# Window attention into a mixture of attention experts: scores as 64-key products, one transfer a unit for q and k, all masks on GpSimd, the gate in PSUM, new step lists

## The chip, the cores and the metric

The kernel runs on one core of a Trainium2 chip. The metric is the device time of one execution in microseconds. Engines are named as in the profile: PE is TensorE (PEld its weight loads), DVE VectorE, ACT ScalarE, POOL GpSimd, SP SyncE, which only issues transfers here.

## The reference

Two attentions follow one another. The first is a sliding window of 32 to either side over 8 batches x 8 heads x 576 positions x 64 dimensions, in fp32:

```python
scores = scale * np.matmul(q, k.transpose(0, 1, 3, 2))
mask = np.abs(pos[:, None] - pos[None, :]) <= 32
attn = softmax(np.where(mask, scores, -1e9))
x = (attn @ v) -> (8, 576, 512)
```

The second is a mixture of four causal attention experts on x: a gate `logits = x @ w_gate` picks the best two of four experts per position and weighs them by a softmax over the two; each expert computes `q, k, v = x @ wq[e], x @ wk[e], x @ wv[e]` (head dimension 64), causal softmax attention over all 576 positions, and a projection `@ wo[e]` back to 512. The output is the weighted sum, (8, 576, 512).

## The kernel before

**The order is written out.** The string ORDER lists 917 steps. A step's name gives its function, its batch and further indices, after a colon an engine (v DVE, g POOL, a ACT), after @ the PSUM banks it uses. The program walks the list once and emits each step's instructions on their engines; every engine runs its own instructions strictly in that order and waits by semaphores for what it needs. A load also waits for the last PE instruction that stands before it in the list (`load` adds that dependency), so a load does not run ahead of its place. PSUM is one tensor of eight banks; who holds a bank follows from the list.

**Window attention of batch b, unit (b, g) with g a group of four heads:**

- `lq`, `lk` load q and k of a unit, `lv` loads V. For q and k the unit's tile has 128 partitions, 32 for each head. `load_qk` knows two layouts. The one used throughout here lays rows 64 m + 2 p + o on partition p, and issues four transfers, one a head, with runs of 512 bytes; for batch 0 in two parts (rows 0 to 319 and 320 to 575). Part letters: `t` issues from ACT's queue, no letter from SP's. The other layout (letters `e`, `f`) lays rows 18 p + o on partition p; then a unit is one contiguous transfer with 4,608 bytes a partition. It is in the code and unused by the list.
- `tq`, `tk` (L298): DVE transposes 32 x 32 blocks, two instructions a unit and tensor, so that the 32 partitions of a head hold half of the head dimension and the columns are positions in order. The output's inner step is 2 elements (18 in the other layout).
- `sc(b, g, half)`: scores, transposed, for half the query columns (288): keys on PSUM partitions, queries as columns; four heads on four row groups of the array (32 rows of a half head dimension), one PSUM bank a head, two accumulating products for the two halves `dh`. Each fp32 product is two PE instructions. Block lists BLK say which keys meet which queries: an entry (par, m, n, lo, hi) takes n keys from 128 m + 64 par against columns lo to hi, on PSUM partitions from 64 par.
- `ex` (L336): ACT takes the exponential of two banks (128 x 576) into SBUF. `mk` (L340): multiplication by the window's mask, on POOL or DVE as the list says.
- `av`: probabilities times V with a column of ones, `un` divides (DVE), `xt` transposes on PE, `xf` copies out of PSUM, `xb` casts to bf16. `vc` copies values on chip so that each 64-key block has its neighbour.

**Experts of batch b,** pair j of experts: `ga` gate logits, `gt`, `ge`, `gm`, `gu` the choice and weights (small tensors of 20 columns; transposed logits LT, differences L2, exponentials EX and numerators NU in SBUF); `pp`/`pe` project q and k, `pv`/`ve` v; `ps` scores, `xe` exponential on ACT, `se` (L511) causal part zeroed on POOL; `po` values, `oe` (L544 to L546) division and gate weight; `pt`, `ot` transposition; `py`, `ye`, `st` output.

All matmuls are recorded at L179, PE transpositions at L182, loads at L185, copies at L171 (ACT) and L173 (DVE, POOL).

**Around the change.** The list starts with `s_mask s_pads lq100`, so the q of batch 1 goes first on SP; the first score step is sc010 and the first value product av02. Buffers hold three units of q and k and of probabilities.

Of the kernel before, what the change touches and what calls it, by code (L numbers as in the profile page):

```python
# [32 lines left out]
    cw0:g av03@2 av04@0 mk1011:g un04@0 sc111@46 un03@2 ex1111@6 cw1:v xt02@0 lw2 cw2:g xt01@2 xf01:v@2 xb01:v  # L33
    lq200 lk200 xf02:a@0 xb02:v mk1001:g ex1110@4 xt00@6 xf00:a@6 sc110@04 ga0@6 gt0@6 xb00:a ex1101@4 lv10
    pp001@2 lv12 ex1100@0 mk1100:g lv11 lq210 pp000@0 pe000:v@0 pe001:a@2 pp010@2 pe010:v@2 mk1101:g mk1111:g
    ps003@0 ps000@4 xe003@0 se003 ps002@6 pv00@0 xe000@4 xe002@6 pp011@4 tq200 vc11:g ve00:a@0 pe011:a@4 ps001@6
    xe001@6 tk200 sc200@02 ex2001@2 ps013@4 lv14 xe013@4 mk1110:v lk210 vc10:v lk300 ps010@6 xe010@6 ex2000@0 ge0
    mk2000:g sc201@24 se000 ex2011@4 ex2010@2 se001 ps012@6 tq210 av12@0 mk2011:g un12@0 av10@4 mk2010:g lq300
    pv01@3 xe012@6 ve01:a@3 gm0 lk310 av13@6 av11@0 un10@4 un13@6 un11@0 se012 av14@4 un14@4 tk210 xt11@6 lw3
    xf11:a@6 lv23 xb11:g xt12@0 xf12:v@0 xb12:g xt10@4 lv22 mk2001:g xf10:v@4 xb10:v lv20 ps011@2 xe011@2 sc211@06  # L40
    ex2111@6 ex2110@0 mk2110:v se002 sc210@24 pp110@6 ex2100@2 mk2100:g ex2101@4 lv21 lq310 cw3:g pe110:a@6 gu0
    mk2101:g pp101@2 pe101:a@2 po00@6 pp100@2 tk300 lv24 oe00@6 pp111@4 se011 pt00@6 pe100:v@2 ps102@2 ps103@0
    pe111:a@4 xe102@2 xe103@0 tq300 ga1@7 gt1@7 lq400 ot00:a@6 mk2111:v sc301@24 ex3010@2 ex3011@4 ge1 tk310
    sc300@06 ex3001@6 ps100@2 xe100@2 lk400 tq310 vc21:g se010 av23@4 vc20:g av22@6 un23@4 ex3000@0 pv11@2 un22@6
    ve11:a@2 av20@0 un20@0 av24@7 lk410 un24@7 se013 ps111@4 xe111@4 mk3011:g ps101@2 lv31 xe101@2 av21@0 un21@0
    sc311@46 ex3110@4 tq400 lv30 sc310@02 ex3111@6 xt21@4 lq410 lv44 ex3100@0 mk3100:g ex3101@2 mk3101:g tk400
    xt20@0 xf21:v@4 xt22@2 po01@6 xf20:a@0 xf22:v@2 ps110@4 oe01@6 ps113@0 ga2@2 gt2@2 xb22:v xe113@0 lv33
    mk3110:v xe110@4 gm1 sc401@06 ex4011@6 mk3010:v tk410 lv32 tq410 ex4010@0 xb21:g sc400@24 mk3001:g lv34
    ex4000@2 mk4000:v lv41 ex4001@4 pv10@6 lv42 lq500 pt01@5 ot01:v@5 lv40 ve10:a@6 xb20:g pp200@3 pe200:a@3
    pp210@0 vc30:a pp201@6 gu1 pe210:a@0 pe201:v@6 pv20@4 ps203@6 lk500 ve20:v@4 ps112@0 mk3111:v xe203@6 xe112@0  # L50
    se100 gm2 ps200@2 xe200@2 mk3000:g lv43 vc31:g av31@6 pv21@5 ve21:v@5 un31@6 av30@0 mk4001:g av33@2 un30@0
    un33@2 mk4010:g lv53 se103 av32@4 un32@4 py02@0 ye02:a@0 av34@7 un34@7 lq510 py01@2 xt32@7 ye01:v@2 xf32:a@7
    xb32:v xt31@4 tk500 xf31:a@4 lk510 sc410@06 ex4100@0 sc411@24 ex4111@4 ex4101@6 py00@0 ex4110@2 vc41:g vc40:g
    se101 ye00:a@0 tq500 tq510 lv52 lv50 xt30@4 xf30:v@4 pp211@6 se102 po10@2 oe10@2 pe211:a@6 ps210@6 ps211@4
    ga3@0 gt3@0 lv54 xe210@6 xe211@4 sc500@26 ex5001@6 ex5000@2 se110 sc501@04 ex5011@4 mk4111:v ex5010@0 mk5001:v
    se112 se111 se113 po11@6 oe11@6 lk600 ps201@4 xb30:g mk4100:g lv51 mk4101:g ps212@2 xe201@4 xe212@2 av41@0
    un41@0 av40@6 ps213@4 xe213@4 mk4011:g un40@6 ge3 ps202@0 mk4110:g av44@2 lq600 tk510 se201 xe202@0 un44@2
# [12 lines left out]
    ex6111@4 pp500@6 pp501@0 pe500:a@6 se313 se310 pt21@2 ot21:a@2 po31@4 ps402@6 xe402@6 pe501:v@0 oe31@4 tq710  # L70
    sc701@02 ex7011@2 st10 ex7010@0 mk6011:v sc700@46 ex7000@4 ex7001@6 ga5@2 ps503@3 xe503@3 ps501@0 ps500@6
    gt5@2 lv74 xe501@0 py22@5 ye22:v@5 vc60:g mk6100:g av61@3 un61@3 pv51@0 ve51:v@0 se411 xe500@6 mk6111:g
    mk6110:g av63@1 un63@1 av62@3 pv41@0 ve41:a@0 un62@3 av60@6 un60@6 mk7001:g ps403@3 ps413@0 xe413@0 xe403@3
    se403 mk7011:g lv70 av64@2 un64@2 ps400@0 ps410@4 ps502@6 pv50@2 xe400@0 xe502@6 xe410@4 se401 se402 ve50:v@2
    xt60@6 xt61@4 lv72 xf60:a@6 pt31@3 xb60:a xt62@2 xf61:v@4 xf62:v@2 ot31:a@3 py20@6 xb61:a ye20:v@6 se400
    po40@0 pp510@2 pe510:a@2 vc70:a xb62:g st20 pt30@7 se410 oe40@0 se500 py21@5 ot30:v@7 ga6@4 gt6@4 gm6 se413
    ye21:a@5 st21 st22 gm5 sc710@02 ex7100@0 sc711@46 ex7110@4 mk7110:v pp511@0 ge5 mk7100:g py30@4 ex7101@2
    mk7101:v pe511:v@0 ex7111@6 mk7111:v vc71:g py31@2 po41@6 oe41@6 pp601@0 ye30:a@4 pp600@4 pe600:v@4 se501
    ye31:a@2 pe601:a@0 mk7000:v ps510@0 ps513@6 xe513@6 se513 st30 se502 pp610@2 xe510@0 pt41@4 pt40@5 pe610:a@2
    se503 ge6 ot41:v@4 ps601@0 ot40:v@5 xe601@0 mk7010:g ps602@6 ps600@2 av71@4 un71@4 xe600@2 av70@0 se601 pv61@2  # L80
    ve61:a@2 un70@0 se600 av73@4 xe602@6 py42@0 py32@1 av72@2 un73@4 ye32:v@1 ps512@4 xe512@4 ps511@6 un72@2
# [14 lines left out]
def kernel(  # L96
# [20 lines left out]
    NQT = 5  # L117
# [194 lines left out]
    def vc(c, b, par):  # L312
# [317 lines left out]
```

## Time and profile before

| | |
|---|---|
| device time, three runs | 266.94, 266.94, 265.85 us (median 266.94) |
| span of the profiled execution | 262.5 us (its own device time is not given; the median is 4.4 us more) |
| PE busy | 228.9 us (87%) |
| DVE / ACT / POOL busy | 193.2 / 147.0 / 127.2 us |
| granted PE clock, mean | 0.975 |
| transfers | 89362 packets, 40.60 MB, 155 GB/s |

Busy time of PE is the union of pipelined matmuls whose ends are modelled, so PE may be busy and yet not at its peak. In the groups of instructions the columns are: line, engine, operation, output<-inputs, shapes, count | busy us, mean ns of one | idle us of the engine just before them and what ended it.

### The profile page before, as it was taken

Reading aid. Unit: us, or ns where it says so; the run is one execution under the profiler, and the core shown is the slowest. Engines: PE = TensorE matmul, PEld = TensorE weight load, DVE = VectorE, ACT = ScalarE, POOL = GpSimd, SP = SyncE. Lnnn points to the kernel's source line nnn. Section 1 sums busy time; section 2 is a strip of 40 time slices with the busy share of each in tenths; the row PEclk is TensorE's granted clock in tenths of the full one; section 3 lists DMA queues with packets and bytes.
Section 4 is the critical chain, followed back from the end, with each engine's and each line's share of the span. In section 5 each row is a group of like instructions: output and inputs, shape, how many; then the busy total and the mean of one; then the engine's idle time right before and its main releaser. Section 6 shows DMA issues by size and latency. Waiting matters only on the chain.

```text
span 262.5 us, 11479 instructions
## 1 busy us (share of the span) xinstructions
PE 228.9 (87%) x5013; PEld 183.2 (70%) x5024; DVE 193.2 (74%) x400; ACT 147.0 (56%) x221; POOL 127.2 (48%) x165
## 2 busy tenths in 40 slices
PE   0286999985989999699989999998899989999981
PEld 0165898664768888567878877886688758877650
DVE  2455896759899889998997956986876596667640
ACT  0223416761646557326745677776657657785852
POOL 5019706765686097337967906109734236322400
PEclk9995699999999999999999999999999999999997
DMA  8969989999974598886186798990021520124366
GB/s 166 209 171 180 228 160 211 204 198 226 199 177 138 161 209 176 170 196 162 34 205 201 157 162 159 216 290 15 2 63 42 186 80 2 32 92 157 126 216 208
DMA packets 89362, 40.60 MB, mean 155 GB/s; under 512 B 47072, under 2 KB 84960, under 8 KB 89312
## 3 DMA queue, kind: packets, MB, share of 16 engines
q1 hardware_dynamic: 86752, 38.69, 64.4%
q10 hardware_dynamic: 2560, 1.18, 2.4%
q8 instruction: 39, 0.64, 1.1%
q14 instruction: 11, 0.09, 0.1%
HBM read 30.42 MB, written 9.44 MB: 152 GB/s over the span
## 4 chain that ended last, share of the span: by engine, by line
PE 64%; DVE 16%; DMA 9%; issue 3%; ACT 3%; SPq 2%; POOL 1%; ACTq 0%; DVEq 0%
PE PS L179 57%; PE PS L182 7%; DVE A L340 5%; DMA qn<-in_q_dram 4%; DMA kn<-in_k_dram 4%; SPq L185 2%; ACT A L336 2%; DVE Tkn L298 1%; DVE RG L545 1%; DVE OE L546 1%; DMA out_dram<-Y 1%; DVE XN L368 1%; POOL V L173 1%; DVE Tqn L298 1%; DVE VE L173 1%
## 5 line engine op out<-in xcount | busy, mean ns | idle before, releaser
L179 PE MATMUL PS<-Tqn,Tkn 32*64 32x96 f32 (+5 forms) x2048 | 63.6, 307 | 16.9 <-DVE Tqn L298 11.6
L340 POOL TENSOR_TENSOR A<-A,MASKP 128x576 f32<-128x576 f32 x41 | 59.2, 1458 | 33.1 <-ACT A L336 32.5
L179 PEld LDWEIGHTS PS<-Tqn,Tkn 32*64 32x64 f32 (+1 forms) x2048 | 51.9, 158 | 29.4 <-DVE Tqn L298 12.0
L336 ACT ACTIVATE A<-PS 128x576 f32<-128x576 f32 x64 | 38.9, 650 | 41.0 <-PE PS L179 41.0
L506 ACT ACTIVATE ATE<-PS 128x1024 bf16<-128x1024 f32 x48 | 47.4, 1023 | 8.4 <-PE PS L179 6.8
L511 POOL TENSOR_SCALAR_AFFINE_SELECT ATE<-ATE 128x256 bf16<-128x256 bf16 (+1 forms) x80 | 31.4, 413 | 39.6 <-ACT ATE L506 24.2
L179 PE MATMUL PS<-V,A 128*64 128x65 f32 (+1 forms) x1280 | 39.6, 222 | 3.8 <-DVE XN L368 2.4
L179 PEld LDWEIGHTS PS<-V,A 128*64 128x64 f32 (+1 forms) x1280 | 36.1, 132 | 7.5 <-DVE XN L368 2.9
L173 POOL COPY V<-V 64x2048 f32<-64x2048 f32 (+1 forms) x12 | 21.8, 1820 | 27.3 <-DMA V<-in_v_dram 21.9
L298 DVE STREAM_TRANSPOSE Tkn<-kn 128x576 f32<-128x576 f32 (+2 forms) x36 | 23.2, 686 | 8.4 <-DMA kn<-in_k_dram 7.3
L298 DVE STREAM_TRANSPOSE Tqn<-qn 128x576 f32<-128x576 f32 (+2 forms) x36 | 23.2, 686 | 7.6 <-DMA qn<-in_q_dram 6.6
L340 DVE TENSOR_TENSOR A<-A,MASKP 128x576 f32<-128x576 f32 x23 | 25.3, 1109 | 3.0 <-ACT A L336 3.0
L368 DVE TENSOR_TENSOR XN<-PS,RC 128x512 f32<-128x512 f32 x32 | 22.1, 691 | 1.1
L179 PE MATMUL PS<-WV,XTB 128*128 128x256 bf16 (+1 forms) x192 | 18.8, 255 | 1.1 <-DVE OTT L173 0.8
L179 PE MATMUL PS<-WO,OTT 128*128 128x512 bf16 (+1 forms) x85 | 18.2, 341 | 1.4 <-ACT OTT L171 0.7
L179 PE MATMUL PS<-XTB,WK 128*128 128x288 bf16 x128 | 18.3, 286 | 1.0 <-DVE QKE L173 1.0
L182 PE MATMUL PS<-ident,XN 128*128 128x128 f32 x144 | 18.1, 275 | 1.1 <-DVE XN L373 0.9
L171 ACT COPY Y<-PS 128x1024 f32<-128x1024 f32 (+1 forms) x17 | 13.7, 826 | 9.3 <-PE PS L179 8.3
L179 PE MATMUL PS<-XTB,WQ 128*128 128x288 bf16 x128 | 18.1, 287 | 0.0
L179 PE MATMUL PS<-QKE 64*128 64x64 bf16 (+4 forms) x192 | 16.8, 277 | 1.4 <-DVE QKE L173 1.2
L182 PEld LDWEIGHTS PS<-ident,XN 128*128 128x128 f32 x144 | 15.8, 141 | 3.1 <-DVE XN L373 1.7
L179 PEld LDWEIGHTS <-ATE 128*128 128x128 bf16 x480 | 16.4, 97 | 2.2 <-POOL ATE L511 0.8
(71 smaller groups left out, 279.8 us busy)
## 6 DMA issues: line engine op xcount, KB each, us to landing
V<-in_v_dram SPq DMA_DIRECT2D x32, 256.0 KB, 4.7
out_dram<-Y SPq DMA_DIRECT2D x16, 512.0 KB, 3.8
qn<-in_q_dram SPq DMA_DIRECT2D x56, 144.0 KB, 4.3
kn<-in_k_dram SPq DMA_DIRECT2D x56, 144.0 KB, 4.3
V<-in_v_dram SPq DMA_DIRECT2D x8, 128.0 KB, 4.2
out_dram<-Y SPq DMA_DIRECT2D x16, 64.0 KB, 2.6
kn<-in_k_dram ACTq DMA_DIRECT2D x8, 80.0 KB, 3.5
qn<-in_q_dram SPq DMA_DIRECT2D x8, 80.0 KB, 2.8
```

What stands on the lines that cost most here:

```text
L171: nc.scalar.copy(o, i)
L173: eng(c).tensor_copy(o, i)
L179: last_pe[0] = nc.tensor.matmul(*a, **kw)
L182: last_pe[0] = nc.tensor.transpose(*a)
L185: r = q_.dma_start(o, i)
L298: nc.vector.transpose(T[:, 64 * m0:64 * m1].rearrange("q (m p o) -> q m o p", p=32, o=2), n_[:, 2 * m0:2 * m1, 32 * dh:32 * dh + 32].rearr ...
L336: nc.scalar.activation(AT[(2 * b + g) % NAT_][half][p], two(b0)[:, :, 0:HS], EXP, scale=scale_att)
L340: eng(c).tensor_tensor(out=ap, in0=ap, in1=MASK[:, None, HS * half:HS * half + HS].to_broadcast([128, 2, HS]), op=MULT)
L368: nc.vector.tensor_tensor(out=XN[T // 2][:, T % 2, :].rearrange("p (g h d) -> p g h d", g=2, h=4), in0=u[:, :, :, 0:64], in1=rc[:, :, :, N ...
L506: nc.scalar.activation(chunk(A, ch), two(b0), EXP, scale=scale_moe)
L511: nc.gpsimd.affine_select(ap, ap, pattern=[[0, n], [1, w]], compare_op=IS_GE, fill=0.0, base=0, channel_multiplier=-1)
L545: nc.vector.tensor_tensor(out=rg, in0=GG[b % 2][:, 2 * j:2 * j + 2, :], in1=rg, op=MULT)
```

## The change

1. **Scores.** Every product has 64 keys. An entry of BLK becomes (par, m, dh, lo, hi), the two head halves are entries of their own, and entries of the lower and the upper 64 PSUM partitions stand in turn: with four row groups that is eight tiles of the array. A step has 40 products instead of 32; columns outside the window of a 64-key block are no longer computed.
2. **q and k.** From batch 1 on, every unit's q and k are loaded with letter `e`: one transfer each, and transposed with an output step of 18. Batch 0 keeps the four transfers a part.
3. **Masks.** All 64 `mk` steps are on POOL (41 before, 23 on DVE).
4. **Gate.** Transposed logits, differences, exponentials and numerators lie in free columns (192 to 432) of the gate's PSUM bank, which stays taken from `ga` to `gu`; LT, L2, EX and NU are gone. `oe` writes its reciprocal in place in PSUM.
5. **Lists.** ORDER is new throughout, with the same 917 steps but for engines and queues. Other moves in it: evacuations `pe` 23 on ACT and 9 on DVE (18 and 14 before); no wide cast `xb` on DVE (3 before), 10 on POOL (7 before); `vc` 12 on POOL and 4 on ACT (2 on DVE and 2 on ACT before); wide `ye` 8 on ACT and 8 on DVE (12 and 4 before). The mask and the pads are made after the first scores.

```diff
 ORDER = """
-    s_mask s_pads lq100 lk011:t tk011:t lk001:t tk001:t lq011 lq001 tq011 lq002 lk012:t lk002:t lq012 s_ones
-    sc010@02 lv02 lk100 lv01 lv03 s_warm tq001 sc000@46 ex0101@2 ex0001@6 mk0001:g ex0000@4 lv00 s_ident mk0101:g
-    tk002:t tk012:t tq002 sc001@24 ex0011@4 mk0011:g mk0000:g tq012 sc011@46 ex0111@6 tq100 tk100 mk0111:g lq110
-    ex0100@0 ex0110@4 vc00:v ex0010@2 mk0010:v lk110 sc101@06 mk0110:v ex1011@6 tq110 ex1010@0 mk1010:v lv04 lw1
-    sc100@24 vc01:g av02@0 tk110 lv13 ex1001@4 un02@0 mk0100:g av01@4 un01@4 av00@6 un00@6 lw0 ex1000@2 mk1000:v
...
+    lk011:t lq002 s_ones lq011 lq001:t lk001 tq011:v tq002:v tk011:v tq001:v tk001:v lk012:t lv00 lk002 s_warm tk012:v
+    tk002:v s_pads lk100:e sc010@02 lq012:t lv03 lq100:e lv02 sc000@46 ex0000@4 ex0100@0 ex0101@2 s_mask lv01 sc001@40
+    lq110:e lk110:e tk100:e lv04 tq012:v ex0001@6 lw0 sc011@26 ex0010@4 ex0011@0 tq100:e sc100@04 lw1 lk200:e lw2
+    mk0000:g mk0100:g mk0011:g mk0001:g ex0111@6 ex0110@2 lq200:e sc101@26 ex1001@4 tq110:e mk0010:g s_ident mk0101:g
+    vc00:g mk0110:g vc01:a mk0111:g av01@4 ex1010@2 ex1011@6 tk110:e lv13 un01@4 ex1000@0 av02@2 av00@6 un00@6 un02@2
...
-    GS = {nm: many(2, [128, NQT, 4], F32, nm) for nm in ("L2", "EX", "GE", "LZ", "PK", "NU")}
+    GS = {nm: many(2, [128, NQT, 4], F32, nm) for nm in ("GE", "LZ", "PK")}
...
-    BLK = [[(0, 1, 128, 96, 288), (0, 0, 64, 0, 96), (1, 0, 64, 0, 160), (0, 2, 64, 224, 288)],
-           [(0, 2, 128, 288, 416), (0, 3, 64, 352, 480), (1, 3, 64, 416, 576), (0, 4, 64, 480, 576)]]
+    BLK = [[(0, 0, 0, 0, 96), (1, 0, 0, 0, 160), (0, 0, 1, 0, 96), (1, 0, 1, 0, 160),
+            (0, 1, 0, 96, 224), (1, 1, 0, 160, 288), (0, 1, 1, 96, 224),
+            (0, 2, 0, 224, 288), (1, 1, 1, 160, 288), (0, 2, 1, 224, 288)],
+           [(0, 2, 0, 288, 352), (1, 2, 0, 288, 416), (0, 2, 1, 288, 352), (0, 3, 0, 352, 480),
+            (1, 2, 1, 288, 416), (0, 3, 1, 352, 480), (1, 3, 0, 416, 576),
+            (0, 4, 0, 480, 576), (1, 3, 1, 416, 576), (0, 4, 1, 480, 576)]]
...
-        for par, m, n, lo, hi in BLK[half]:
+        for par, m, dh, lo, hi in BLK[half]:
             k0 = 128 * m + 64 * par
-            for dh in range(2):
-                for hh in range(4):
-                    r = slice(32 * hh, 32 * hh + 32)
-                    mm(PS[64 * par:64 * par + n, bank[hh], lo - c0:hi - c0], K[dh][r, k0:k0 + n], Q[dh][r, lo:hi],
-                       start=(dh == 0), stop=(dh == 1), skip_group_check=True)
+            for hh in range(4):
+                r = slice(32 * hh, 32 * hh + 32)
+                mm(PS[64 * par:64 * par + 64, bank[hh], lo - c0:hi - c0], K[dh][r, k0:k0 + 64], Q[dh][r, lo:hi],
+                   start=(dh == 0), stop=(dh == 1), skip_group_check=True)
...
+    def gate(b0, n):
+        if n:
+            return PS[:, b0, 352 + 20 * n:372 + 20 * n].rearrange("p (t e) -> p t e", e=4)
+        return PS[:, b0, 192:352].rearrange("p (t x) -> p t x", x=32)
+
     def gt(c, b, b0):
         i = b % 2
-        nc.vector.transpose(LT[i][:, :, :], one(b0)[:, 0:160].rearrange("p (t x) -> p t x", x=32))
-        L = LT[i][:, :, 0:4]
+        nc.vector.transpose(gate(b0, 0), PS[:, b0, 0:160].rearrange("p (t x) -> p t x", x=32))
+        L = gate(b0, 0)[:, :, 0:4]
...
-        nc.vector.tensor_tensor(out=GS["NU"][i], in0=GS["EX"][i], in1=GS["PK"][i], op=MULT)
+        nc.vector.tensor_tensor(out=gate(b0, 3), in0=gate(b0, 2), in1=GS["PK"][i], op=MULT)
...
-        nc.vector.reciprocal(rg, p_[:, :, :, 64])
-        nc.vector.tensor_tensor(out=rg, in0=GG[b % 2][:, 2 * j:2 * j + 2, :], in1=rg, op=MULT)
+        nc.vector.reciprocal(p_[:, :, :, 64], p_[:, :, :, 64])
+        nc.vector.tensor_tensor(out=rg, in0=p_[:, :, :, 64], in1=GG[b % 2][:, 2 * j:2 * j + 2, :], op=MULT)
```

More of the change, by code (lines that the diff above doesn't have):

```diff
@@ L33 @@
[L33 to L57, printed above, removed]
@@ L92 @@
+    py70@2 py72@4 st62 ye70:a@2 ye72:v@4 st71 st70 st72
 """
@@ L436, in gm, with gu @@
         nc.vector.tensor_tensor(out=GS["PK"][i], in0=L, in1=bc(GV["m2"][i]), op=IS_GE)
-    def gu(c, b):
+    def gu(c, b, b0):
         i = b % 2
-        nc.vector.tensor_tensor(out=GS["NU"][i], in0=GS["EX"][i], in1=GS["PK"][i], op=MULT)
-        nc.vector.tensor_reduce(GV["su"][i], GS["NU"][i], axis=AXX, op=ADD)
+        nc.vector.tensor_tensor(out=gate(b0, 3), in0=gate(b0, 2), in1=GS["PK"][i], op=MULT)
+        nc.vector.tensor_reduce(GV["su"][i], gate(b0, 3), axis=AXX, op=ADD)
         nc.vector.reciprocal(GV["su"][i], GV["su"][i])
-        nc.vector.tensor_tensor(out=GG[i][:, :, :].rearrange("p e t -> p t e"), in0=GS["NU"][i],
+        nc.vector.tensor_tensor(out=GG[i][:, :, :].rearrange("p e t -> p t e"), in0=gate(b0, 3),
                                 in1=bc(GV["su"][i]), op=MULT)
```

103 lines of the change are left out of this document (62 added, 41 removed).

## The prediction

> **What bounds the kernel now.** I read the page first (span, busy shares, chain, costliest groups), then windows, then the chain in order of time.
>
> ```profile
> span 262.5 us, 11479 instructions
> PE 228.9 (87%) x5013; PEld 183.2 (70%) x5024; DVE 193.2 (74%) x400; ACT 147.0 (56%) x221; POOL 127.2 (48%) x165
> PE 64%; DVE 16%; DMA 9%; issue 3%; ACT 3%; SPq 2%; POOL 1%; ACTq 0%; DVEq 0%
> PE PS L179 57%; PE PS L182 7%; DVE A L340 5%; DMA qn<-in_q_dram 4%; DMA kn<-in_k_dram 4%; SPq L185 2%; ACT A L336 2%; DVE Tkn L298 1%; DVE RG L545 1%; DVE OE L546 1%; DMA out_dram<-Y 1%; DVE XN L368 1%; POOL V L173 1%; DVE Tqn L298 1%; DVE VE L173 1%
> L179 PE MATMUL PS<-Tqn,Tkn 32*64 32x96 f32 (+5 forms) x2048 | 63.6, 307 | 16.9 <-DVE Tqn L298 11.6
> ```
>
> PE is the bound: 87% busy, 64% of the chain that ended last. Its largest group is the scores, 63.6 us. The page gives no device time of its own execution; the runs beside it have a median of 266.94 us, 4.4 us more than the span. I sum against 262.5 and add 4.4.
>
> The timeline of PE shows where the value products begin, and windows cut there and at two places further on what the engines do (length, then busy of PE, PEld, DVE, ACT, POOL, then granted clock, DMA share, GB/s):
>
> ```profile
> 31.59 0.63 PE L179 MATMUL PS<-V,A 128*64 128x65 f32 x14
> ```
> ```profile
> 0.00:31.59 31.59, 16.76 (x384) 13.66 (x385) 17.12 (x45) 7.45 (x12) 16.12 (x22) 0.84 0.91 190
> 31.59:70.85 39.26, 34.48 (x856) 28.25 (x853) 30.38 (x55) 19.46 (x31) 21.25 (x23) 1.00 1.06 199
> 70.85:240.00 169.15, 161.68 (x3562) 130.78 (x3567) 135.84 (x276) 107.07 (x161) 85.81 (x109) 1.00 0.56 131
> 240.00:262.50 22.50, 16.00 (x221) 10.52 (x221) 9.88 (x29) 12.99 (x17) 4.04 (x12) 0.94 0.58 206
> ```
>
> Up to 31.59 the kernel does six of 32 score steps (384 of 2048 instructions) and mostly waits for loads. From 31.59 to 70.85 (the first products of batch 1's second expert group) PE has 4.8 us idle, with DVE at 77%. From 70.85 to 240 PE is 96% busy, 7.5 us idle: there only less PE work helps. The end is a chain through the last batch.
>
> **The score step.** It becomes 40 products of 64 keys instead of 32, two instructions each (2048 over 32 steps is 64). One pair of steps, cut where 128-key products change to 64-key products:
>
> ```profile
> 67.45:70.85 3.40, 3.40 (x128) 2.87 (x128) 0.00 (x0) 1.00 1.14 206
> 67.45:68.11 0.66, 0.66 (x16) 0.54 (x17) 1.00 0.84 230
> 68.11:69.13 1.02, 1.02 (x53) 0.90 (x49) 1.00 0.97 193
> 69.13:69.99 0.86, 0.86 (x19) 0.64 (x17) 1.00 1.31 227
> 69.99:70.85 0.86, 0.86 (x52) 0.79 (x49) 1.00 1.39 184
> ```
>
> A step is 1.70 us. The 128-key blocks have 128 and 192 columns and four turns each (two head halves, two instructions): 0.66 and 0.86 us. So 64 columns x 4 turns are 0.20 us, 0.78 ns a column and turn, and 0.26 us is entry. The 64-key stretches (48 instructions each) run the two output halves side by side; by the longer half they should take 0.26 + 224 x 4 x 0.78 = 0.96 (measured 1.02) and 0.26 + 160 x 4 x 0.78 = 0.76 (measured 0.86). Columns explain them up to 0.10.
> After the change either half of a step has 288 columns on each side (96+128+64 or 64+128+96 against 160+128): 288 x 4 x 0.78 = 0.90, one entry instead of two, 0.26, and 0.10 on top: 1.26 us, 0.44 less. Below lies 0.90 (no entry), above 2.13, if an instruction costs what the mean one of the pair does (80 x 3.40/128). I take 1.26, near the lower end, since columns explain all four stretches. 26 steps come after 31.59, so A = -11.4 us, bounds -20.8 and +11.2.
>
> [...]
>
> **The start.** The chain in order of time, and POOL's first masks:
>
> ```profile
> 1.26 3.93 DMA kn<-in_k_dram
> 5.57 2.95 DMA kn<-in_k_dram
> 8.54 2.75 DMA kn<-in_k_dram
> 11.30 2.85 DMA qn<-in_q_dram
> 14.80 3.13 PE PS L179 x48
> ```
> ```profile
> 18.68 1.41 POOL L340 TENSOR_TENSOR A<-A,MASKP 128x576 f32<-128x576 f32 x1 [13.91 <-ACT A L336]
> 20.93 4.16 POOL L340 TENSOR_TENSOR A<-A,MASKP 128x576 f32<-128x576 f32 x3
> ```
>
> Loads go in generations; four follow one another before the products at 14.80. Now SP begins with batch 1's q (lq100). In the new list that goes behind batch 0, and sc000 needs three generations: about 11.3, then two transpositions, a step and its exponential, 3.3: first mask at about 14.6 instead of 18.68. But all eight masks of batch 0, the identity (0.8, the hole in the second row pair) and a value copy now stand in POOL's one queue ahead of the first value product:
>
> ```profile
> L340 POOL TENSOR_TENSOR A<-A,MASKP x41: 1393/1413/1923, 18.7 to 218.7; 128x576 f32<-128x576 f32 x41
> L340 DVE TENSOR_TENSOR A<-A,MASKP x23: 709/750/2480, 27.1 to 216.7; 128x576 f32<-128x576 f32 x23
> L433 DVE TENSOR_TENSOR GE<-LT,m x8: 165/170/1461, 58.9 to 234.7; 128x20 f32<-128x20 f32 x8
> ```
> ```profile
> L173 POOL COPY V<-V 64x1536 f32<-64x1536 f32 x4 | 5.9, 1468 | 2.0 <-DMA qn<-in_q_dram 1.9
> L511 POOL TENSOR_SCALAR_AFFINE_SELECT ATE<-ATE 128x256 bf16<-128x256 bf16 x64 | 25.9, 427 | 24.8 <-ACT ATE L506 24.2
> L173 POOL COPY V<-V 64x2048 f32<-64x2048 f32 x8 | 16.0, 1996 | 25.3 <-DMA V<-in_v_dram 21.9 <-DMA qn<-in_q_dram 3.3
> L511 POOL TENSOR_SCALAR_AFFINE_SELECT ATE<-ATE 64x128 bf16<-64x128 bf16 x16 | 5.7, 355 | 14.8 <-ACT ATE L508 14.4
> L173 POOL CAST XTB<-XTF 128x1024 bf16<-128x1024 f32 x7 | 7.3, 1036 | 5.9 <-ACT XTF L171 4.0 <-DVE XTF L173 1.9
> L298 DVE STREAM_TRANSPOSE Tkn<-kn 128x576 f32<-128x576 f32 x28 | 20.0, 754 | 3.8 <-DMA kn<-in_k_dram 2.7 <-PE PS L179 1.1
> L336 ACT ACTIVATE A<-PS 128x576 f32<-128x576 f32 x64 | 38.9, 650 | 41.0 <-PE PS L179 41.0
> L220 DVE MEMSET QKE<- 128x64 uint32 x3 | 0.3, 112 | 0.0
> L213 DVE MEMSET V<- 128x64 f32 x2 | 0.2, 112 | 0.0
> ```
>
> 8 x 1.413 + 0.8 + 1.47 = 13.6, so the first value product at about 28.2: B = -3.4 us. Bounds -6 (it waits for the six steps alone) and +3 (the loads gain nothing, masks from 18.7 on without DVE's help: 32.3, and one late exponential).
>
> **Masks on POOL.** 23 masks leave DVE (23 x 1.109 = 25.5) and cost POOL 23 x 1.413 = 32.5 us. The POOL and DVE rows (minimum, median, maximum) show DVE instructions on two SBUF operands blown up from 0.17 to 1.46 and from 0.71 to 2.48. In the new kernel none is left: masks, casts and value copies leave DVE, and the gate's operands lie in PSUM. DVE comes to about 150 us. Where DVE's time goes from the path, POOL is late next. From first value product to first products of batch 1's second group, the new list has the same six score steps, ten value steps and transpositions, four projections of batch 0; PE has 34.48 - 6 x 0.44 = 31.8 us. POOL has 15 masks (21.2), three wide casts (3.1), two value copies (3.5), seven causal pieces (2.9), WQ's cast and the small ones (1.8): 32.5. POOL is the longer one there. I keep the idle 4.8 on top: 37.3 instead of 39.26, so this stretch gains 2.0, not 2.6. From 70.85 to 240 POOL has 41 masks (57.9) and some 50 us of the rest in 160 us; cover for PE is the lead of the units, so zero, bounds 0 and 7 x 1.41 x 2 (two late masks a batch).
>
> **Transfers and transpositions.** 112 issues of q and k become 28 from batch 1 on. Their waits on the chain after the start are two:
>
> ```profile
> 50.46 3.88 DMA qn<-in_q_dram
> 61.33 4.05 DMA qn<-in_q_dram
> ```
>
> PE runs on beside them but for tenths (4.8 us idle in all that stretch), so I book nothing, bounds -4 and 0. The transposition now writes every 18th element instead of every second. I keep 754 ns: setting 64 scattered elements (V's ones, 65 apart) took 112 ns, as long as 64 adjacent ones (QKE's pad). Upper bound: twice the time, 56 x 0.754 = 42 us of DVE.
> [...]
>
> **Gate, division, copies.** Gate operations at their undisturbed 0.17 cost DVE less; the PSUM bank stays taken through a chain of eight short operations, covered by seven other banks: zero. ACT gets five evacuations of q and k, two value copies and some small ones more and four output copies less:
>
> ```profile
> L171 ACT CAST QKE<-PS 128x576 bf16<-128x576 f32 x18 | 11.4, 641 | 9.0 <-PE PS L179 7.6 <-DVE su L441 1.4
> L171 ACT COPY V<-V 64x1536 f32<-64x1536 f32 x2 | 2.9, 1472 | 0.0
> L171 ACT COPY Y<-PS 128x1024 f32<-128x1024 f32 x12 | 12.0, 1015 | 4.7 <-PE PS L179 3.7 <-ACT ATE L506 0.9
> ```
>
> 5 x 0.64 + 2 x 1.47 - 4 x 1.02 = +2.1 of 147 us on an engine idle half the time: zero.
>
> **Sum.** 262.5 - 3.4 (start) - 2.0 (to 70.85) - 20 x 0.44 = 8.8 (to 240) - 0 (end) = 248.3; + 4.4 = 252.7 us.
>
> **Rivals.**
> 1. Instructions set the score's pace. For it: 2560 instead of 2048. Against it: 17.9 ns in the best stretch. At 26.6 ns a step is 2.13 us: 262.5 - 3.4 + 26 x 0.43 + 4.4 = 274.7, slower; it outweighs the start from 22.9 ns on. Chance 0.10. [...]
> 2. POOL's queue becomes the bound: causal pieces of one batch wait behind masks of the next. For it: 32.5 against 31.8 above; against it: 48% busy now. One late mask a batch, 7 x 1.41: 262.6; two: 272.4; slower from ten late masks in all. Chance 0.17, half of it slower.
> 3. ACT: two exponentials of a step (2 x 0.65 = 1.30) outlast it (1.26), so the banks of a pair come free late. At 0.7 us for eight pairs: 258.3. For it: today a step leaves 0.4 us; against it: ACT idle half the time. Chance 0.10.
> 4. Transpositions take twice as long; they hold 2% of the chain, so +5.3: 258.0. Chance 0.06. [...]
> 5. Otherwise as summed, 245 to 259: chance 0.57.
>
> A measurement of this kernel tells 0.5% from no change. Faster: 0.57 + 0.10 + 0.06 + half of rival 2, 0.81; same 0.04; slower 0.15. Low end: scores at 0.90 (-9.4) and the start's bound (-2.6) give 241; the high end reaches into rival 2: 266.
>
> **What will show it.** Score steps of 1.2 to 1.3 us and about 45 us in their group; first value product near 28; POOL near 160 us, masks near 1.41; transpositions at 0.75; no DVE mask; PE near 215 us. I am wrong if score steps stay at 1.7, if PE waits for masks (A on POOL) by more than a few us, or if the idle time in 70.85 to 240 grows.

## The result, and the profile after

| | time, median (lowest to highest) | profiled execution: its time, span |
|---|---|---|
| before | 266.54 us (263.76 to 268.46) | not given, 262.5 us |
| after | 270.39 us (266.24 to 277.34) | 272.21 us, 270.5 us |

The ratio of after to before is 1.0103, 95% interval 1.0063 to 1.0143: the change makes the kernel about 1% slower, where 252.7 us was forecast. Ratios, here and below, are over the fast executions alone (of after the ten of 20 that lie within 1.5% of its fastest, so not the profiled one), and medians are over all executions, which is why those of the table stand at 1.0144 to one another.

The page of the changed kernel: busy shares, the chain that ended last by engine and by line, then the rows of the masks, the scores and a transposition.

```profile
span 270.5 us, 12380 instructions
PE 224.7 (83%) x5526; PEld 180.3 (67%) x5536; DVE 172.4 (64%) x353; ACT 153.1 (57%) x241; POOL 156.1 (58%) x192
...
PE 72%; DMA 11%; issue 8%; DVE 4%; ACT 3%; ACTq 0%; SPq 0%; DVEq 0%
...
L341 POOL TENSOR_TENSOR A<-A,MASKP 128x576 f32<-128x576 f32 x64 | 89.5, 1413 | 37.5 <-ACT A L337 36.9
L177 PE MATMUL PS<-Tqn,Tkn 32*64 32x128 f32 (+3 forms) x2560 | 52.5, 297 | 28.7 <-issue 11.2
...
L292 DVE STREAM_TRANSPOSE Tkn<-kn 128x576 f32<-128x576 f32 x28 | 32.6, 1243 | 5.1 <-PE PS L177 3.2
```

PE has 4 us less work than before and yet the span is 8 us longer. DVE has 21 us less work, POOL 29 us more, and neither has much of the chain (DVE 4%, against 16% before; POOL none). What is new is "issue", 8% of the chain against 3% before: time in which the engine waited for nothing that the profile shows. Windows over two undisturbed stretches of scores (one step, then a pair) and over one disturbed step show what that is worth (length, busy PE and its instructions, granted clock, DMA share, GB/s):

```profile
99.40:100.69 1.29, 1.29 (x82) 1.00 0.81 304
120.50:122.98 2.48, 2.48 (x162) 1.00 0.05 10
144.80:148.90 4.10, 1.61 (x81) 1.00 0.89 303
```

Left alone, a step of 80 instructions takes 1.24 to 1.29 us, as forecast (1.26). The third takes 4.1 us, at full clock, with 1.61 us of work in it. The timeline of PE there, and the pieces of "issue" over 2 us in the chain of the changed kernel (start, length):

```profile
144.82 0.68 PE L177 MATMUL PS<-Tqn,Tkn 32*64 32x64 f32 x33
148.00 0.99 PE L177 MATMUL PS<-Tqn,Tkn 32*64 32x128 f32 x47 [2.49 <-issue]
```
```profile
26.96 3.46 issue
...
38.35 3.40 issue
...
81.49 2.11 issue
...
145.51 2.49 issue
```

PE stops in the middle of a step, with operands and banks in hand. The waits (us in total, times, longest), first of before, then of after, show in these rows crumbs of at most 0.4 us before and stops of up to 4.1 us after:

```profile
PEld PS L179 <- issue: 8.9, 36, 0.4
...
PE PS L179 <- issue: 0.2, 1, 0.2
```
```profile
PEld PS L177 <- issue: 25.9, 25, 4.1
...
PE PS L177 <- issue: 18.7, 14, 3.5
```

What PE waits for is its own program. The page's part on DMA queues has a row for it (kind "instruction"), which I had passed over: 39 packets before, 43 after. Its row in before, then the rows of after:

```profile
q8 instruction: 39, 0.64, 1.1%
```
```profile
q1 hardware_dynamic: 56736, 38.68, 52.1%
q10 hardware_dynamic: 2560, 1.18, 1.9%
q8 instruction: 43, 0.70, 1.1%
```

Each is a packet of 16,384 bytes, and PE (with PEld) executes 256 instructions between one and the next, so 64 bytes an instruction. In before, PE and PEld execute 10,048 instructions, 39.3 blocks of 256; in after 11,072, 43.3. From the packet records and the starts of PE's instructions (in us from the span's start), four of the blocks:

```
after, packet no. (from 0)       1              3              11             24
packet on its way          27.38-28.72    39.00-40.28    81.22-82.30   145.68-146.62
PE's start behind the hole     30.42          41.75          83.60          148.00
distance of PE's starts         3.93           3.62           2.38            2.76
```

In each PE runs dry about 449 instructions past the start of a block (counted from PE's first recorded instruction: in after at 449, 705, 961, 1217 and so on, always whole blocks of 256 further, to one instruction), and goes on 1.3 to 1.7 us after the late packet has landed. Below, a **hole** is a distance of over 0.35 us between two starts of PE without a semaphore wait that ends within 2 us of the landing of such a packet. Before has none. After has 13, together 22.0 us. The forecast span was 248.3 us; 248.3 + 22.0 = 270.3, and 270.5 was measured.

That these meet is partly luck, for other terms of the forecast are off too (below), and the granted clock costs time that neither number holds. Between 31.59 and 240 us before had the full clock, 1.00 in both rows of the prediction. In after four stretches of 3.41 us stand at half of it (length, busy PE, PEld, DVE, ACT, POOL, then granted clock, DMA share, GB/s):

```profile
43.34:46.75 3.41, 3.41 (x18) 3.22 (x16) 1.24 (x4) 1.85 (x2) 1.10 (x3) 0.50 0.00 0
84.30:87.71 3.41, 3.41 (x65) 3.41 (x66) 0.90 (x2) 1.72 (x4) 1.77 (x2) 0.50 0.89 164
149.16:152.57 3.41, 3.41 (x17) 2.14 (x15) 0.00 (x0) 1.75 (x3) 2.70 (x4) 0.50 0.13 31
179.88:183.29 3.41, 3.41 (x113) 2.79 (x100) 1.46 (x3) 1.51 (x3) 0.44 (x2) 0.50 0.02 5
```

PE is busy all through them. From one product of 288 columns (XTB with WQ) to the next the starts stand 240 ns apart there and 123 elsewhere (medians). If all of PE's work there went by the clock alone, they cost 4 x 3.41 x 0.50 = 6.8 us, an estimate. The first three begin 0.7 to 1.6 us behind the end of a hole of over 2.3 us, the fourth 0.8 us behind two waits of PE for a transposition (1.51 and 0.55 us). But none follows the longest hole (26.50 to 30.42), so what sets them off isn't shown. Over its 20 executions after was granted 0.928 (in the longest, 277.34 us) to 0.981; before, beside the runs below, 0.965 to 0.999.

### The profile page after: what moved, and what is told of

It reads as the page before. It is cut to its first block, busy times and chain, and to the rows that moved or that the text cites. A ratio compares the mean times of both kernels' runs of the same rounds, so it can differ in the third digit from the quotient of the medians.

```text
span 270.5 us, 12380 instructions
## 1 busy us (share of the span) xinstructions
PE 224.7 (83%) x5526; PEld 180.3 (67%) x5536; DVE 172.4 (64%) x353; ACT 153.1 (57%) x241; POOL 156.1 (58%) x192
## 3 DMA queue, kind: packets, MB, share of 16 engines
HBM read 30.42 MB, written 9.44 MB: 147 GB/s over the span
## 4 chain that ended last, share of the span: by engine, by line
PE 72%; DMA 11%; issue 8%; DVE 4%; ACT 3%; ACTq 0%; SPq 0%; DVEq 0%
PE PS L177 63%; PE PS L180 9%; DMA qn<-in_q_dram 4%; DMA out_dram<-Y 3%; DMA kn<-in_k_dram 2%; DMA V<-in_v_dram 1%; ACT A L337 1%; DVE Tkn L292 1%; DVE Tqn L292 1%; ACT Y L169 1%; DVE Y L171 0%; ACT VE L169 0%; ACTq L183 0%; ACT WV L169 0%; ACT WK L169 0%
## 5 line engine op out<-in xcount | busy, mean ns | idle before, releaser
L341 POOL TENSOR_TENSOR A<-A,MASKP 128x576 f32<-128x576 f32 x64 | 89.5, 1413 | 37.5 <-ACT A L337 36.9
L177 PE MATMUL PS<-Tqn,Tkn 32*64 32x128 f32 (+3 forms) x2560 | 52.5, 297 | 28.7 <-issue 11.2
L177 PEld LDWEIGHTS PS<-Tqn,Tkn 32*64 32x64 f32 x2560 | 44.9, 148 | 35.7 <-issue 19.1
L292 DVE STREAM_TRANSPOSE Tkn<-kn 128x576 f32<-128x576 f32 x28 | 32.6, 1243 | 5.1 <-PE PS L177 3.2
L292 DVE STREAM_TRANSPOSE Tqn<-qn 128x576 f32<-128x576 f32 x28 | 32.2, 1242 | 3.0 <-PE PS L177 1.9
L171 POOL CAST XTB<-XTF 128x1024 bf16<-128x1024 f32 (+1 forms) x18 | 12.5, 706 | 18.5 <-DVE XTF L171 6.9
L169 ACT COPY XTF<-PS 128x128 f32<-128x128 f32 (+1 forms) x23 | 13.4, 632 | 16.4 <-PE PS L180 13.3
L169 ACT CAST QKE<-PS 128x576 bf16<-128x576 f32 x23 | 14.4, 642 | 9.3 <-PE PS L177 9.1
L177 PE MATMUL PS<-VE,ATE 128*128 128x65 bf16 x480 | 17.5, 193 | 2.7 <-issue 1.5
L171 DVE COPY Y<-PS 128x1024 f32<-128x1024 f32 (+1 forms) x12 | 11.5, 956 | 12.7 <-PE PS L177 10.5
```

The lines of the kernel that those rows point to most:

```text
L169: nc.scalar.copy(o, i)
L171: eng(c).tensor_copy(o, i)
L177: last_pe[0] = nc.tensor.matmul(*a, **kw)
L292: nc.vector.transpose(T[:, :].rearrange("q (p o) -> q o p", o=18)[:, o0:o1], n_[:, o0:o1, 32 * dh:32 * dh + 32])
L341: eng(c).tensor_tensor(out=ap, in0=ap, in1=MASK[:, None, HS * half:HS * half + HS].to_broadcast([128, 2, HS]), op=MULT)
```

## The experiments

Two things could make a block late: PE goes through 256 instructions faster (**pace**: a score step issues 160 instructions for PE and PEld in 1.26 us, where it issued 128 in 1.70), or the packet waits behind transfers of q, k and V (**contention**, also called backlog below). The runs were timed in four sets of three rounds, each beside the kernel before, whose medians were 265.6 to 267.3 us. "New list" means everything of the change but what is named. Ratios are to before, with the 95% interval; holes come from each run's trace. (The expectations below use a narrower count of holes: 14.0 us for a_plain, 8.4 for a_noload.)

| run | list | transfers of q, k | scores | us | ratio | holes, us |
|---|---|---|---|---|---|---|
| before | old | 4 a unit, 512 B runs | 128-key | 265.6-267.3 | 1 | 0 |
| b_scores | old | as before | 64-key | 267.49 | 1.0033 (0.9978-1.0089) | 11.9 |
| b_e | old | 1 a unit | 128-key | 282.09 | 1.0586 (1.0497-1.0676) | 2.3 |
| after | new | 1 a unit | 64-key | 270.39 | 1.0103 (1.0063-1.0143) | 22.0 |
| a_oldsc | new | 1 a unit | 128-key | 265.27 | 0.9939 (0.9893-0.9984) | 4.7 |
| a_noload | new | 1 a unit, none from batch 2 on | 64-key | 253.02 | 0.9517 (0.9450-0.9585) | 9.3 |
| a_noload_old | new | the same | 128-key | 261.03 | 0.9819 (0.9756-0.9883) | 0 |
| a_plain | new | as before | 64-key | 260.72 | 0.9786 (0.9720-0.9852) | 14.5 |
| ap_oldsc | new | as before | 128-key | 259.83 | 0.9797 (0.9747-0.9848) | 4.3 |
| ap_mix5 | new | as before | 64-key from batch 5 | 259.89 | 0.9794 (0.9697-0.9891) | 6.2 |
| a_heads | new | 4 a unit, 4,608 B runs | 64-key | 261.03 | 0.9785 (0.9713-0.9857) | 13.1 |
| ah_oldsc | new | the same | 128-key | 261.46 | 0.9834 (0.9742-0.9925) | 2.0 |
| ah_mix5 | new | the same | 64-key from batch 5 | 263.12 | 0.9877 (0.9776-0.9978) | 6.1 |
| a_pad | new | 1 a unit, 512 B runs | 64-key | 263.55 | 0.9884 (0.9803-0.9965) | 17.4 |
| ap_spread | new | as before, set apart | 64-key | 268.98 | 1.0103 (1.0037-1.0169) | 18.3 |
| aps_old | new | as before, set apart | 128-key | 271.39 | 1.0166 (1.0089-1.0243) | 3.6 |
| a_gate | new, gate in SBUF | as before | 64-key | 267.85 | 1.0104 (1.0059-1.0148) | 13.9 |

### The parts: transfers back, scores alone, transfers alone

a_plain: the changed kernel without the letters `e`, so that q and k come in four transfers a unit and are transposed with output step 2.

```diff
-    tk002:v s_pads lk100:e sc010@02 lq012:t lv03 lq100:e lv02 ...
+    tk002:v s_pads lk100 sc010@02 lq012:t lv03 lq100 lv02 ...
```

> The changed kernel with q and k of batch 1 on loaded and transposed as before (four transfers a unit, runs of 512 bytes, output step 2); list, scores, masks and gate stay new. Backlog theory (PE's instruction fetch waits behind the large q and k transfers) and run-length theory (it waits behind runs of 4,608 bytes): the holes of PE beside a fetch go from 22 us to under 2, span about 248, 250 to 253 us. Pace theory (PE simply uses its instructions faster than they can be fetched): holes stay above 15 us, 266 to 272 us. The transpositions go back to 0.75 us each under all.

b_scores: the kernel before with the new BLK and `sc` alone.

```diff
-    BLK = [[(0, 1, 128, 96, 288), (0, 0, 64, 0, 96), ...
+    BLK = [[(0, 0, 0, 0, 96), (1, 0, 0, 0, 160), ...
```

> The kernel before with nothing changed but the score blocks (64-key products on eight tiles); old list and old loads. Backlog and run-length theories: no holes beside fetches, score steps of about 1.3 us, 26 x 0.4 us less where PE is the bound: 255 to 259 us. Pace theory: holes beside fetches appear at the score steps, at least 5 us of them, 262 to 270 us.

a_heads: the layout of `e`, with one transfer a head.

```diff
-            load(t[:, o0:o1, :]..., src[b, 4 * g:4 * g + 4]..., queue)
+            for h in range(4):
+                load(t[32 * h:32 * h + 32, o0:o1, :]..., src[b, 4 * g + h]..., queue)
```

> The changed kernel with each unit's q and k in four transfers, one a head (32 partitions), runs still 4,608 bytes, transposition unchanged (step 18). Eight transfers in flight are then a quarter of the bytes. Backlog theory: holes beside fetches mostly gone (under 5 us), 250 to 256 us, transpositions still 1.24 us. Run-length theory: holes stay at 15 us or more, 264 to 272 us. Pace theory: the same as run length.

a_pad: one transfer a unit, into a padded tile, so that it is cut into runs of 512 bytes.

```diff
-    NAT = {nm: many(NNAT, [128, 18, 64], F32, nm) for nm in ("qn", "kn")}
+    NAT = {nm: many(NNAT, [128, 9, 144], F32, nm) for nm in ("qn", "kn")}
```

> The changed kernel with one transfer a unit, but the tile padded so that every run is 512 bytes; transposition step 18 as in the changed kernel. Backlog theory: holes stay at 15 us or more, 264 to 272 us. Run-length theory: holes under 5 us, 250 to 256 us. Pace theory: holes stay.

b_e: the kernel before with letter `e` for q and k from batch 1 on.

```diff
-    s_mask s_pads lq100 lk011:t ... tq100 tk100 ...
+    s_mask s_pads lq100:e lk011:t ... tq100:e tk100:e ...
```

> The kernel before with q and k from batch 1 on as one transfer a unit (letter e), its score blocks and all else as before. Backlog: holes of 5 to 10 us come, and DVE has 27 us more of transpositions off the path: 270 to 276 us. Pace: no holes above 0.35 us, 265 to 267 us, or up to 270 if DVE's transpositions are waited for.

Taking back the transfers alone turns 1% slower into 2.1% faster. a_heads shows that long runs alone aren't the reason: same runs, same step of 18, a quarter of the bytes in each transfer, and 9.4 us less than after. But a_pad, one transfer with short runs, is 6.8 us under after too, with 17.4 us of holes. In four transfers the runs make 0.3 us (a_heads against a_plain), in one they make 6.8: it is the large transfer with the long runs that costs most, and why is open. The scores alone in the old list with the old transfers bring nothing (1.0033): 11.9 us of holes stand against the 11.4 us that the steps should gain. So pace makes holes with no large transfer of q or k about.

The one large transfer alone in the old list costs 5.9%, and not by holes (2.3 us). Its page gives busy time, chain, DVE's masks and a transposition:

```profile
PE 235.7 (84%) x5024; PEld 187.4 (67%) x5024; DVE 215.8 (77%) x400; ACT 147.2 (53%) x221; POOL 126.1 (45%) x165
...
PE 53%; DVE 30%; DMA 6%; issue 5%; ACT 2%; ACTq 0%; DVEq 0%
```
```profile
L294 DVE STREAM_TRANSPOSE Tkn<-kn 128x576 f32<-128x576 f32 x28 | 32.5, 1240 | 0.5 <-PE PS L179 0.5
L340 DVE TENSOR_TENSOR A<-A,MASKP 128x576 f32<-128x576 f32 x23 | 27.6, 1207 | 2.7 <-ACT A L336 2.6
```

With 23 masks on DVE (27.6 us) the slower transpositions (754 to 1240 ns) are on the chain: DVE has 30% of it, 16% before, and the transpositions 10% (2% before). In the new list, without DVE's masks, the same transpositions cost next to nothing: a_heads (1243 ns) and a_plain (756 ns) differ by 0.3 us. This fits a layout of `e` that needs the masks gone from DVE; no run moved the masks alone.

### Contention or pace: loads left out, and the old scores, in the new list

```diff
     def load_qk(nm, src, b, g, part, c):
+        if b >= 2:
+            return
...
     def lv(c, b, m):
+        if b >= 2:
+            return
```

> The changed kernel with the loads of q, k and V of batches 2 to 7 left out (the steps that use them run as before, on what batches 0 and 1 left in the buffers, so the output of those batches is not the reference's). Theory contention (PE's instruction block comes late because the transfers of q, k and V in flight take the DMA engines): the holes before about 60 us stay, about 7.5 us of the 22; behind them none above 0.35 us; 270.4 - 14 = 256 us, and 2 to 4 less where a load was waited for: 252 to 257. Rival pace (PE with 64-key scores goes through 256 instructions faster than a block can be had, whatever else moves): holes of 18 to 22 us stay, 266 to 271 us.

a_noload_old and a_oldsc put the score blocks of before into a_noload and into the changed kernel; ap_oldsc into a_plain.

```diff
-    BLK = [[(0, 0, 0, 0, 96), (1, 0, 0, 0, 160), ...
+    BLK = [[(0, 1, 128, 96, 288), (0, 0, 64, 0, 96), ...
```

> The run a_noload (loads of q, k and V of batches 2 to 7 left out, 253.0 us, holes 8.4 us, all before 40 us) with the score blocks of before. If the 64-key scores bring their gain where the blocks of instructions come in time, this is slower: 26 steps by 0.44 us is 11.4, less the early holes that the slower steps avoid (8.4 to about 2): 253.0 + 11.4 - 6 = 258 us. If the scores' gain is lost to something else than the transfers in flight, it is the same, 252 to 254 us.

> The changed kernel with the score blocks of before (32 products a step) in the new list. Score steps 1.70 us again, 26 steps x 0.44 = 11.4 us more of PE. Pace: the slower steps leave the fetch its time, holes fall from 22 to under 8 us, 270.4 + 11.4 - 14 = 268 us. Contention alone: holes stay near 20 us and 270.4 + 11.4 = 282 us. Between these by the share of the two.

> The run a_plain (the new list with the old transfers of q and k, 260.7 us, holes 14.0 us) with the score blocks of before. If the holes come of pace and contention together, they fall to under 4 us: 260.7 + 11.4 - 10 = 262 us, so that the 64-key scores bring about 1 us. If of contention alone: 14 us stay, 272 us, and the scores bring their full 11.4 us.

With the loads of batches 2 to 7 out, the chain of a_noload has two pieces of "issue" over 1 us, both while the loads of batches 0 and 1 are under way:

```profile
26.82 3.75 issue
...
38.50 1.76 issue
```

Of its 9.3 us of holes 8.4 lie before 40 us. Behind stands one, 0.85 us at 115.4: its packet was on the way from 113.05 to 114.73, with the DMA engines 92% busy from 113 to 114, and what SP had issued last were output stores (from 109.92 on). With the old scores and all loads the holes fall to 4.7 us. So it takes both: fast steps and transfers in flight. The four corners:

| new list, one transfer a unit | 128-key scores | 64-key scores | the scores bring |
|---|---|---|---|
| all loads | 265.27 | 270.39 | 5.1 us slower (4.4 by the ratios) |
| loads only for batches 0 and 1 | 261.03 | 253.02 | 8.0 us faster |

The mechanism that the forecast rests on, cheaper score steps, is real and worth 8 us, but only where PE's blocks mostly come in time. With all loads and the old transfers it is worth nothing (ap_oldsc 259.83, a_plain 260.72). a_oldsc came 2.7 us below its expectation, with fewer holes than allowed for; a_noload_old came 3 us above, which I did not take apart. (The profiled execution of a_noload, which its holes are from, took 256.55 us and was its longest.)

How late a block is can be read from the packet records: from the moment at which PE has executed 165 instructions of a block, the next packet starts after about 1.0 to 1.3 us (median) wherever the loads' queue kept the DMA engines under 30% busy in the microsecond behind that moment, in before, after, a_plain, a_heads, a_oldsc and a_noload alike. Where it kept them over 70% busy the median is 1.2 us in before, 1.6 in a_oldsc, 2.3 in a_heads, 2.7 in a_plain and 3.8 in after. (165 is a mark for counting; that the packet is asked for just there isn't shown.) It has landed about 1.1 us later, and in none of before, after, a_plain, a_noload and a_oldsc does PE start an instruction past the 449 sooner than 1.25 us behind the landing. So with the DMA engines idle some 3.5 us lie between the mark and PE's first use of the packet, and in that time PE must not have gone through 284 further instructions. In pure score steps of 160 these last 2.2 us (284/160 x 1.26), with 128 in 1.70 us they last 3.8. By this estimate the old steps leave just enough time, and the new ones don't, even with the DMA engines idle, if all 284 are scores. Behind its first stretch a_noload has at most two steps (320 instructions) in a row, and no hole there falls on scores.

### Setting the transfers apart

ap_spread takes a_plain's four transfers of a unit apart, up to three steps of the list between one and the next (nine from first to last; the 49 of the expectation was wrong); aps_old is the same with the old scores.

```diff
-    ... lk200 lw2 mk0000:g mk0100:g ...
+    ... lk2000 lw2 mk0000:g mk0100:g ... lk2001 ... lk2002 ... lk2003 ...
```

> The run a_plain (new list and scores, old transfers; 260.7 us, holes 14.0 us) with the four transfers of a unit from batch 1 on set apart in the list, each waiting for a later PE instruction, up to 49 steps apart, instead of one behind the other. Theory (a block waits for the bytes in flight): less in flight at a time, holes 5 to 9 us, 255 to 258 us. Rival (the number of transfers in the queue over the whole time counts, not their bunching): holes stay 12 to 15 us, 260 to 262 us.

> ap_spread with the score blocks of before. ap_oldsc, the same without setting apart, had 259.8 us and holes of 4.3 us. If setting apart takes the holes, 32 products a step gain only what is left of 4 us: 257 to 260 us, and the 64-key scores of ap_spread come out ahead by 2 to 4 us. Rival: 259 to 261 us and no difference between the two.

Neither theory held. Holes rose to 18.3 us, and with the old scores, where they fell to 3.6, the time was no better (271.39). The chain by engine, first of a_plain, then of ap_spread:

```profile
PE 73%; DMA 12%; issue 5%; DVE 4%; ACT 2%; SPq 1%; ACTq 0%; DVEq 0%
```
```profile
PE 67%; DMA 12%; issue 6%; DVE 5%; SPq 4%; ACT 4%; POOL 1%; DVEq 0%; ACTq 0%; POOLq 0%
```

SP's own queue has 4% of it instead of 1%: each piece now waits in SP for a later PE instruction, and every load behind it in the queue waits with it. Why the holes rose by 4 us rather than stayed isn't settled.

### The gate

a_gate: a_plain with the gate's small tensors in SBUF.

```diff
-        nc.vector.transpose(gate(b0, 0), PS[:, b0, 0:160]...)
+        nc.vector.transpose(LT[b % 2], PS[:, b0, 0:160]...)
```

> a_plain with the gate's transposed logits, differences, exponentials and numerators in SBUF again (the in-place reciprocal of the normaliser stays). The prediction put this part at nothing: 260 to 261.5 us. Rival: work in PSUM is slower for DVE and ACT on a chain that PE waits for, 258 to 259.5 us.

Neither expectation held: back in SBUF it is 7.1 us slower, for a part that the prediction had put at zero. Two of its operations, first in a_plain (PSUM), then in a_gate (SBUF):

```profile
L439 DVE SCALAR_TENSOR_TENSOR LZ<-GE,PS 128x20 f32<-128x20 f32 x8 | 1.4, 175 | 0.3
L430 DVE TENSOR_TENSOR PS<-PS,m 128x20 f32<-128x20 f32 x8 | 1.5, 188 | 0.3
```
```profile
L438 DVE SCALAR_TENSOR_TENSOR LZ<-GE,LT 128x20 f32<-128x20 f32 x8 | 7.5, 940 | 0.3
L429 DVE TENSOR_TENSOR L<-LT,m 128x20 f32<-128x20 f32 x8 | 6.8, 847 | 0.3
```

Twenty columns take 175 ns with one operand in PSUM and up to 940 ns on average with both in SBUF beside 64 masks on POOL; DVE's busy time goes from 147.9 to 167.6 us, and its share of the chain from 4% to 12%. Of the 16 instructions in the last two rows eight took 178 to 181 ns. The other eight took 253 to 3921 ns, and each ended 32 to 38 ns behind the end of an instruction of POOL: a mask, a value copy or a causal piece. So these eight end with POOL's work; by what means POOL holds them up isn't shown.

### What was still open: the slower transpositions, and 64-key scores where the loads have thinned out

ah_oldsc puts the old score blocks into a_heads. ap_mix5 and ah_mix5 use them for batches 0 to 4 of a_plain and a_heads, and the 64-key blocks for batches 5 to 7 (`sc1` is `sc` of before with its blocks).

```diff
     def sc(c, b, g, half, b0, b1):
+        if b < 5:
+            return sc1(c, b, g, half, b0, b1)
```

> The run a_heads (a unit in four transfers, one a head, runs of 4,608 bytes, output step 18; 261.0 us) with the score blocks of before. a_oldsc, one transfer a unit, had 265.3 us; ap_oldsc, the old transfers and output step 2, 259.8. If those 5.5 us are the one large transfer, this has 259 to 261 us; if they are the 27 us of slower transpositions on DVE, 264 to 266 us.

> a_plain with the score blocks of before for batches 0 to 4 and the 64-key blocks for batches 5 to 7, whose score steps mostly stand after the transfers of q and k have thinned out. If the gain of the 64-key scores is lost only where transfers hold the blocks of instructions up, 12 steps gain 12 x 0.44 = 5.3 us on ap_oldsc's 259.8, less holes of 1 to 2 us that stay: 255 to 257 us. If the gain is lost there too: 259 to 261 us.

> a_heads with the same mixture of score blocks. By the same sum from ah_oldsc's time, 4 to 5 us less than that run: 255 to 257 us where that has 260. If the gain is lost there too: as ah_oldsc.

ah_oldsc lies 3.8 us under a_oldsc and 1.6 over ap_oldsc: most of the 5.5 us is the one large transfer, what is left for the transpositions is within the intervals. The mixtures didn't bring what I expected. The ten stretches with the score steps of batches 5 to 7 take 20.2 us in ap_mix5 against 22.6 in ap_oldsc, 2.4 of the 5.3 us; the kernel as a whole gained nothing. One of its stops, from PE's timeline:

```profile
187.89 1.12 PE L177 MATMUL PS<-Tqn,Tkn 32*64 32x64 f32 x59
190.06 0.55 PE L177 MATMUL PS<-Tqn,Tkn 32*64 32x96 f32 x21 [1.04 <-issue]
```

No transfer of q or k was in flight there, but SP had issued a load of V at 183.72 and an output store at 184.19, and the DMA engines were full from 185 to 187 (shares of 0.96 and 1.11). PE had 3.46 us for its 284 instructions, value products and scores in a row, and the packet landed after 3.39 (about 2.1 where the DMA engines were under 30% busy). That was too late by the time that lies between a landing and PE's next start: PE went on 1.40 us behind it. So a block came late with only transfers other than those of q and k about. That the 64-key scores gain is thus shown only with the loads left out, not in any complete kernel.

The fastest complete kernels are ap_oldsc, ap_mix5, a_plain and a_heads, at 0.978 to 0.980 of before, not told apart by their intervals.

## Why the prediction was wrong

**The step that failed: part A, "26 steps come after 31.59, so A = -11.4 us".** Its price holds (1.24 to 1.29 us a step where nothing disturbs it). What failed is the assumption that PE is always handed its instructions. Score stretches behind the first run took 46.7 us before, 44.0 in after and 36.4 in a_noload, so 10.3 us of the 11.4 are there when the blocks come in time and 2.7 when they don't. The holes behind the first run that don't fall on scores fall on value products and on the experts' products. Over the whole kernel the 64-key scores brought 0.9 us more (a_plain against ap_oldsc) and 5.1 us more (after against a_oldsc) where 11.4 less was booked.

**"Transfers: I book nothing, bounds -4 and 0."** Wrong, and outside the bounds: against a_plain the single transfers cost 9.7 us, of which 7.5 are holes (22.0 against 14.5). The path that I looked for, a wait of PE for q or k, wasn't it; the transfers hit PE through its program.

**Transpositions, "I keep 754 ns".** Mis-sized: 1243 ns, 27 us more of DVE, so 172.4 instead of about 150. The memset rows that I went by (112 ns for 64 elements, 65 apart or adjacent) said nothing on transpositions. The cost in the new list was 0.3 us (a_heads against a_plain) or 1.6 (ah_oldsc against ap_oldsc), both within the intervals and less than rival 4's 5.3; in the old list it went on the chain (b_e).

**The start, first value product at 28.2.** It came at 34.4. The first run of scores took 24.0 us with 5.9 us of holes in it; 34.4 - 5.9 = 28.5, and 29.1 in ap_oldsc. The order of loads and masks was read rightly, PE's supply again not.

**Masks on POOL.** Right: 1413 ns each, POOL 156.1 us against "near 160", and no wait of PE for a mask among its rows. Rival 2 didn't come.

**Gate at zero.** Mis-sized: in the new list, beside 64 masks on POOL, it is worth 7 us (a_gate against a_plain); what it is worth against before isn't shown. I had named the mechanism (operands in PSUM, DVE's operations back at 0.17 us) and put it to DVE's account, not to the chain from gate to the expert output.

**4.4 us beside the span.** The profiled executions show 1.7 us between span and time (272.21 and 270.5; in a_plain 260.70 and 259.0): 2.7 us too much.

**The rivals.** Rival 1, instructions that set the pace (274.7, at 0.10), came nearest in its mechanism, but as a price on each instruction it is refuted by 1.29 us a step, 16 ns an instruction (the 17.9 that was held against it is 0.86 us over 48 instructions). The 272.4 of rival 2 (two late masks a batch) lies nearer the measured time, but by luck: PE waited for no mask. The true form, a block of 256 that comes late, wasn't among them. My own sign, "the idle time in 70.85 to 240 grows", was the right alarm: PE is busy 161.68 of 169.15 us there before and 156.41 of 169.10 after. (Three of the stretches at half clock lie in it, so by the estimate above its busy time, too, is longer than the work.)

```profile
70.90:240.00 169.10, 156.41 (x3970) 127.15 (x3973) 117.57 (x235) 108.65 (x178) 109.86 (x130) 0.97 0.47 131
```

## What to carry to other kernels

When an edit makes PE's instructions shorter and more numerous, count them per microsecond against the instruction packets: here a block of 256 had landed about 2.1 us after PE had executed 165 instructions of a block where the DMA engines were idle, and 4.9 us after with transfers of 576 KB in flight, and PE went on with it no sooner than 1.25 us behind the landing. A gain on PE can be lost to transfers that PE never waits for by a semaphore, as here (22.0 us of holes in after); "issue" in the chain and the row of the instruction queue are where this shows. And an operation that is costed at nothing because it is short should be looked up beside what the other engines will do then: one of the gate's took 940 ns on average instead of 175.

## What was not expected of the hardware

- PE's program comes by DMA, on a queue that the page lists beside those of the data (1.1% of the 16 engines' span), in packets of 16,384 bytes, one for 256 instructions (39 for 10,048 instructions before, 43 for 11,072 after). In after PE stopped 13 times about 449 instructions past a block's start and went on 1.3 to 1.7 us behind the landing of the next packet; its starts there stood up to 3.9 us apart. In before no such distance was over 0.35 us.
- Such a packet started later beside one transfer of 576 KB a unit (median 3.8 us behind PE's 165th instruction of a block, with the DMA engines over 70% busy) than beside four of 144 KB with the same runs (2.3), both with the 64-key scores; with the old scores it was 1.6 beside one transfer. Why it started 1.2 us behind that instruction beside the old transfers in the old list and 2.7 in the new one (64-key scores) is open; the new list issues its loads by PE's progress at other places, and what stood in the queues at each was not taken apart.
- Stretches of 3.41 us at half the granted clock fell into the busy middle of after (four) and not of before; three of the four stood just behind a long hole.
- A DVE transposition of 128 x 576 fp32 takes 754 ns with an output step of 2 elements and 1243 with 18; a memset with a step of 65 showed no such price (112 ns for 64 elements either way).
